# Pooled and local attention with a gated product on one core: five per-engine issue orders replaced by five others

## The chip, the cores and the metric

One Trainium2 chip, one of its cores. The metric is the device time of one execution in microseconds (us); of several runs the median is given. The engines are named as in the profile: PE (TensorE matmul), PEld (its weight loads), DVE (VectorE), ACT (ScalarE), POOL (GpSimd) and SP (SyncE, which here only issues DMAs). L880 is line 880 of the kernel.

## What is computed

Shapes: batch 8, heads 8, sequence 576, head dimension 64; all inputs fp32. Four weights (512x1024, 512x1024, 1024x1024, 1024x512) come as 64-bit floats.

```python
q_d, k_d, v_d = (x.reshape(B, H, Sd, 4, D).mean(axis=3) for x in (q, k, v))
out_up = np.repeat(sm_attn(q_d, k_d, v_d), 4, axis=2)      # pooled attention, 144 keys
mask = np.abs(pos[:, None] - pos[None, :]) < 4             # local attention, 7 keys
out_local = softmax(where(mask, scale * q @ k.T, -1e9)) @ v
x = (out_up + out_local).transpose(0, 2, 1, 3).reshape(4608, 512)
out = (((x @ w1) * (x @ w2)) @ w3) @ w_out
```

## The kernel before

The product w3 @ w_out is folded into one 1024x512 matrix W' first (`fold`), so that a token costs two gate products and one down product. Every fp32 operand of these is split into a high and a low fp32r part, and each product is three matmuls, high*high, high*low and low*high (L306, L307, L308).

The tokens are worked in three kinds of steps:

- **Weights.** Each 128-row block of a weight is loaded as raw 64-bit words (`raw`, L331, 512 KB, a ring of six buffers early on), turned into fp32 by ACT (L338, L346) and DVE (L350) and joined by DVE (L353); only the join gives the raw buffer back for the next load. Joined blocks of w_out (`wo`) and w3 (`wx`) feed 64 folding products on PE (L388, two matmuls each), whose sums are split into `wphl` (L398, L399). The gate weights follow the same way (L432, L434).
- **Attention of batches 0 and 1** ("group units" 0 to 5): local scores by PE (L719, `se_ps`), softmax, transposes (L689), values (L768, `oe_ps`). It lies in the first 190 us, beside the weights. The local attention of batches 2 to 7 is done by DVE and ACT in units 6 to 23, three to a batch: seven products `pr<-q_t,kv` (L880) and their sums (L893, on ACT L890), a softmax over seven offsets (L905 to L916), seven products `pv` (L947, on ACT L939) that are added into `xl`, on DVE (L957) or by an accumulating DMA issued by POOL (L955, three to a unit, in a chain), a transpose (L961), the addition of the pooled result (L968), and the split into `xh` and `xl` (L978, L982).
- **Pooled attention**, one batch at a time: its v rows are summed four to one by a plain load (L458 to L460, SP) and three accumulating DMAs (L457, POOL), each after the one before has landed; from batch 2 on q and k likewise (L454, L473). 16 rows of the sum are copied to a second place (`vl`, L477 on DVE for batches 0 and 1). Then scores (L534), softmax with a normalization on POOL (L566), transposes (L577), values (L495, `o_ps`, which reads `vs` and `vl`), and a copy to `oup` (L506).
- **The gated product** in nine chunks of 512 tokens. For each of eight column blocks f: 24 gate matmuls into two `pab` banks, a copy by ACT (`a`, L1034), a multiplication by DVE (L1036), the split `gh` (ACT, L1040) and `gl` (DVE, L1045), then 12 down matmuls into four `acc` banks.

All of this is recorded as 3096 tasks, each on one engine with its dependencies. The order of issue is not computed: the table `ORDER` lists for ACT, DVE, PE, Pool and SP the numbers of that engine's tasks in the order in which they go out, and `Plan.order` (which also merges the five lists into the program's text, by assumed costs) takes the next of a list only. An engine issues strictly in that order, so an instruction that waits holds back all that stand behind it on its engine. On SP and POOL this is the order of the DMA issues.

```python
left[e] = [l[k] for w in ORDER[e].split() for a, _, b in [w.partition("-")] for k in range(int(a), int(b or a) + 1)][::-1]
...
            if left[e] and all(j in end for j in self.pre[left[e][-1]] + self.begun[left[e][-1]]):
...
            i = left[e].pop()
```

Of the kernel before, what the change touches and what calls it, by code (L numbers as in the profile page):

```python
# [69 lines left out]
        "0-1 122 118 120 117 121 2-3 90 119 93 91-92 4 94 97 95-96 5-6 98 7-8 99 123 9 125 127-128 126 124 10-11 100 131 101-102 13 12 "  # L70
        "103 105 104 132-133 130 106 111 107-108 110 109 141 134 142 129 112-113 135 137 144 114 143 14 140 139 136 16 15 138 17-18 "
        "115-116 19 145 21 20 146 22-24 26 25 31-32 151 147 33 29 152 27 149 28 150 35 148 34 186 30 187 153 155-156 189 188 157 154 158 "
        "190 159 37 36 160 191 162 161 166 38 165 163-164 40 167-168 39 42 41 192 195 43 194 197 193 49 196 204 202 205 203 199 52 207 "
        "206 198 201 200 169 48 57 174 173 60 51 170 172 171 53 50 180 175 177-178 65 176 209 208 54 179 68 45 55 181-182 47 56 183 59 62 "
        "58 64 63 67 184 66 185 61 69 44 46 70 212 73 72 71 76 75 74 213 77-78 214 79 215 80-81 216 82-84 297 85-86 217 88 87 218 89 "
        "210-211 219 236-237 235 232 234 233 239 244 243 245 238 220 241-242 247 246 240 248-249 221 253 250-252 256 262 259 263 258 257 "
        "260-261 264-265 222 254-255 223 266-267 224 268-269 271 270 274 272-273 275 225-226 298 300-301 299 296 316 315 320 318 302 317 "
        "303 321 325 323 319 326 322 324 227 304 309 308 306-307 276 327 228 305 277 229 328-329 334 330 335 331 336 332 337 333 338 230 "
        "339 278 231 341 345 342 344 343 346 350-351 348 352 279 347 349 311 310 280 312 281 353 313-314 354-359 282 360 414 361 415 362 "
        "416 363 417 364 283 365 390-392 389 388 397 387 393-395 398 340 396 418 413 419 284-285 420 286 425 399 424 421-423 436 435 434 "  # L80
        "400 432 401 287 402 406 403 407 404 288 405 408 366 409 289 431 410 433 437 439 411 441 440 290 438 442 426-427 291 428 443 367 "
        "444 429 445 430 446 292 447 293 448-449 531 450 533 294 451 461-462 457 459 368 458 532 452 369 453 295 454 412 455 534 370 460 "
        "464 468 463 530 466 465 535 467 536 371 469 372 470-474 537 475 373 476 538-539 541-542 540 477 506 505 507 374 508 478 509 375 "
        "479 504 480 544 510-511 513 543 481 514 456 515 376 512 545 377-378 516 546-547 517-519 379 520-521 648 522 649 651 523 650 524 "
        "550 525 551 526 548 527 552 380 528 549 553 482 381 647 483 652 554 653 559 558 556 555 557 654 659 655-656 658 657 560 382 484 "
        "561-563 383 564 661 660 565 567 384 485 568 578 385 566 486 575-576 579 574 577 569 386 583 570 585 662 571 487 572 584 488 581 "
        "580 529 582 586 489 587-588 490 589-591 663 592 664 593 623 621-622 624 594 573 491 595 626 596 625 597 492 627 598 630 628 632 "
        "629 631 763 493-495 633 764 767 765-766 634 496 635-640 665 641 668 642 666 643 497 599 667 644 498 645 600 669 499 670 768 675 "
        "769 674 671 673 601 676 672 500 602 677 770 774 772 775 771 773 678 501 679 502 680 603 681 711 682 604 713 715 683-684 712 685 "
        "716 686 605 687 714 688 777 776 689 722 646 778 503 721 720 718 717 719 606 723 607 779-780 608-609 724-728 881 729 882 884 883 "  # L90
        "730-732 610 733 741 737 740 738 742 734 746 735 748 611 739 744 747 612 745 743 690 613 880 885 614 886 749-757 615 758 736 759 "
        "616 760 783 761 691 784 786 617 782 618 781 785 791 619 692 620 790 792 693 887 788 889 888 890 892 891 789 787 694 793-795 800 "
        "796 801 797 802 893-894 798 695 803 895 804 799 762 828 696 830 829 697 832-833 831 836 834 837 839 835 838 698 805 896-897 699 "
        "840 700 841-842 701 843-846 702 847 703 848-850 854 851 856 852 855 859 704 857-858 862-863 865 864 861 860 705 806-807 706 866 "
        "808 867-870 707 871 708 872-873 809 874-875 709 876 810 877 710 853 878 899 898 900 811 902 901 812 903 906 909 905 908 907 904 "
        "813-814 910 815 911-917 879 816 918-922 950 948 817 946 945 818 949 947 954 953 955-956 819 952 951 820 957 821 923 822 973 972 "
        "975 924 981 823 982 979 958 964 959 965 960 824-825 961 966 925 967 962 926 826-827 968 963 969 927 976 974 977-978 928 980 971 "
        "929 983 930 984-986 931 987-988 932 989-995 970 933-936 996 937-943 997 944 998-1015"
    ),
    DVE=(  # L100
        "78-79 82-83 80 84 81 86 85 87 113 88 114-115 0 116 97 102 101 98 103 99 1 117 90 89 91 94 92-93 104 95 2 105 96 3 106 118-122 4 "
        "127 123 5-6 128 7 129 107-108 130 124 109 125-126 8-9 160 110 161 111 134 112 162 135-136 164 137 165-166 131-133 100 10-12 "
        "138-140 13-14 141 15 143 142 16 144 17-18 159 19 163 145-147 20 148 25-26 152 27 153 23 154 21-22 171 170 28 172 155 24 167 173 "
        "168 149 169 150-151 174-175 156 176 157 194 183 182 177 184 158 195-196 29 197 185-187 30-31 181 198 178 199 179 200 32 201 180 "
        "33 205 34 206 35 207-208 202-204 189 188 190 44 209-211 40 42 51 191-193 43 41 218 216 214 212 215 213 45 37 46 39 47 49 52 48 "
        "54 53 56 55 58 50 57 36 38 59 61 60 220 63 62 221 65 64 66-67 222-223 68-72 224 73 75 225 76 74 77 226 217 219 227 236-239 "
        "243-246 240-242 247-250 252 251 253 228 254-255 229 256 261 257 262-267 230 258-260 231 268 270 269 271 232 276 272 274 278 273 "
        "275 277 279 298 233 297 299-300 309 301 311 302 313 234 296 312 310 314 316 315 303-304 317 305 319 318 320 235 321-323 280 "
        "324-325 306 326 307 327 308 281 328 330 339 341 340 342-343 329 282 344 332 345-347 331 333 335 349 283 350 348 284 351 334 352 "
        "285 353-357 359 384 414-415 385 416 358 336 386 286 388 417 389 287 418 387 419 337 391 360-361 390 362 364 392 394 338 395 393 "  # L110
        "288 420 396 421 289 422 397 363 398 426 399 428 427 400 430 401 429 423 365 424 402 425 403 290 405 431 291 366 433 292 404 432 "
        "407 293 367 434 436 408 406 437 410 294 435 295 438-444 409 445 447 456 458 533 532 457 534 446 460 449 411 459 368 412 461 369 "
        "462 450 463 370 413 535 448 536 371 537 452 464 466 465 467-468 451 469 372 470-473 373 538-539 474 540 502 476 453 504 506 541 "
        "505 542 374 543 454 503 375 507 475 509 508 510 512 511 513 478 376 455 477 377 479 481 378 514-516 379 517-520 480 651 650 523 "
        "521 544 652 545-546 548 547 522 549 525 550 653 380 654 482 381 655 483 526 524 551 528 552 554 553 656-657 555 658 484 556 485 "
        "557 527 558 382 659 559 660 560 661 561 383 562-563 565 574 529 576 486 578 577 487 575 564 579 567 580-582 584 583 488 530 489 "
        "566 585 568 570 531 586-587 490 588-590 569 491 591-592 594 620 622 624 623 571 593 572 492 596 621 493 625 627-628 494 626 573 "
        "630 597 595 629 599 495 631 496 632 767 633 768 497 634 769 635-638 598 639 641 498 662 770 664 666 600 640 601 643 663 665 499 "
        "602 771 667 500 772 669 642 501 644 646 668 603 670 672 671 673 774 674 645 604 675 773 676 605 677 775 678-679 708 680 709 681 "
        "710 712-713 606 776 683 777 647 607 648 682 714 685 778 711 715 608 716 686 717-718 649 719 684 688 720-721 609 722-725 610-611 "  # L120
# [1096 lines left out]
```

## Time and profile before

| | us |
|---|---|
| three runs | 819.39, 821.57, 822.07 |
| their median | 821.57 |
| the profiled execution, its own time | 821.9 |
| its span, first to last instruction | 819.8 |
| PE busy / DVE busy / ACT busy / POOL busy in the span | 757.4 / 613.3 / 518.3 / 153.6 |
| mean granted TensorE clock, as a share of full speed | 0.965 |

How to read the views: the page's second part cuts the span into 40 slices of 20.5 us and gives a digit for each; a table of stretches gives busy time by engine, the mean granted clock, the busy share of the 16 DMA engines and the data rate; the timeline lists instructions with start, duration and, in brackets, the idle time of the engine before them and what ended it; the list of waits sums such idle times; the chain that ended last follows back, from the last instruction, what released each step. Matmul records overlap their successors, so their starts tell the rate.

### The profile page before, as it was taken

Reading aid. Unit: us, or ns where it says so; the run is one execution under the profiler, and the core shown is the slowest. Engines: PE = TensorE matmul, PEld = TensorE weight load, DVE = VectorE, ACT = ScalarE, POOL = GpSimd, SP = SyncE. Lnnn points to the kernel's source line nnn. Section 1 sums busy time; section 2 is a strip of 40 time slices with the busy share of each in tenths; the row PEclk is TensorE's granted clock in tenths of the full one; section 3 lists DMA queues with packets and bytes.
Section 4 is the critical chain, followed back from the end, with each engine's and each line's share of the span. In section 5 each row is a group of like instructions: output and inputs, shape, how many; then the busy total and the mean of one; then the engine's idle time right before and its main releaser. Section 6 shows DMA issues by size and latency. Waiting matters only on the chain.

```text
span 819.8 us, 13615 instructions
## 1 busy us (share of the span) xinstructions
PE 757.4 (92%) x4672; PEld 573.7 (70%) x4672; DVE 613.3 (75%) x1047; ACT 518.3 (63%) x2033; POOL 153.6 (19%) x187
## 2 busy tenths in 40 slices
PE   3979889999888999898989899998999999999995
PEld 1435458787666867676768687776788888888884
DVE  5748575647999989999799698998799995841111
ACT  3857785655876867878686496688577757422111
POOL 1212113001223332252141423201011100100000
PEclk9979989999998999999989899999999999999998
DMA  6969796012877687778855478643445342421001
GB/s 210 316 175 288 226 247 169 18 36 79 208 170 185 115 217 173 156 137 210 197 91 141 134 153 186 141 98 109 116 116 131 94 116 72 87 38 52 1 0 52
DMA packets 51964, 111.81 MB, mean 136 GB/s; under 512 B 6056, under 2 KB 20392, under 8 KB 51896
## 3 DMA queue, kind: packets, MB, share of 16 engines
q0 software_dynamic: 15360, 38.94, 27.7%
q1 hardware_dynamic: 36400, 71.75, 27.1%
q8 instruction: 37, 0.61, 0.3%
q14 instruction: 31, 0.25, 0.1%
q10 hardware_dynamic: 136, 0.26, 0.1%
HBM read 80.26 MB, written 9.44 MB: 109 GB/s over the span
## 4 chain that ended last, share of the span: by engine, by line
PE 45%; DMA 22%; DVE 15%; issue 7%; ACT 7%; POOL 3%; SPq 1%; POOLq 0%; DVEq 0%; ACTq 0%
PE pab L306 9%; PE pab L308 9%; PE pab L307 9%; DMA vs<-in_v_dram 7%; DMA xl<-pv 6%; PE acc L308 4%; DMA qks<-in_qk_dram 4%; PE acc L306 4%; PE acc L307 4%; DVE pr L880 4%; DVE s_t L893 2%; PE accw L388 2%; DVE pv L947 2%; PE o_ps L495 1%; POOL pexp L566 1%
## 5 line engine op out<-in xcount | busy, mean ns | idle before, releaser
L939 ACT ACTIVATE pv<-kv,s_t 128x64 f32<-128x64 f32 x432 | 116.1, 340 | 21.3 <-DVE s_t L916 12.6
L890 ACT ACTIVATE junk<-pr 128x64 f32<-128x64 f32 x432 | 110.6, 256 | 22.5 <-DVE pr L880 11.6
L308 PE MATMUL acc<-wphl,gl 128*128 128x512 f32 x288 | 115.0, 399 | 5.7 <-DVE gl L1045 5.5
L306 PE MATMUL acc<-wphl,gh 128*128 128x512 f32 x288 | 116.4, 404 | 2.1 <-ACT gh L1040 2.1
L880 DVE TENSOR_TENSOR pr<-q_t,kv 128x768 f32<-128x768 f32 x126 | 116.9, 951 | 1.6 <-DMA q_t<-in_q_dram 1.4
L307 PE MATMUL acc<-wphl,gh 128*128 128x512 f32 x288 | 113.5, 394 | 0.0
L955 POOL DMA_DIRECT2D xl<-pv x54 | 48.5, 899 | 312.6 <-DVE xl L957 228.4
L1036 DVE TENSOR_TENSOR a<-pab,a 128x512 f32<-128x512 f32 x72 | 49.2, 683 | 68.5 <-PE pab L308 54.2
L1040 ACT CAST gh<-a 128x512 fp32r<-128x512 f32 x72 | 44.4, 617 | 67.6 <-DVE a L1036 40.2
L1034 ACT COPY a<-pab 128x512 f32<-128x512 f32 x72 | 42.0, 583 | 66.3 <-PE pab L308 57.0
L893 DVE TENSOR_REDUCE s_t<-pr 128x12 f32<-128x768 f32 x90 | 83.5, 942 | 0.0
L890 ACT ACTIVATION_READ_ACCUMULATOR junk<-pr 128x1 f32 x432 | 80.9, 187 | 0.0
L1045 DVE TENSOR_TENSOR gl<-a,gh 128x512 fp32r<-128x512 f32 x72 | 51.1, 710 | 29.0 <-ACT gh L1040 28.8
L947 DVE TENSOR_TENSOR pv<-kv,s_t 128x768 f32<-128x768 f32 x72 | 69.3, 971 | 1.3 <-DMA xl<-pv 1.1
L308 PEld LDWEIGHTS acc<-wphl,gl 128*128 128x128 f32 x288 | 54.8, 190 | 21.3 <-DVE gl L1045 9.3
L388 PE MATMUL accw<-wo,wx 128*128 128x512 f32 x128 | 64.1, 643 | 4.7 <-DVE wx L353 4.6
L306 PEld LDWEIGHTS acc<-wphl,gh 128*128 128x128 f32 x288 | 54.8, 190 | 16.2 <-ACT gh L1040 3.7
L306 PE MATMUL pab<-xh,wo 128*128 128x512 f32 x144 | 59.6, 414 | 4.1 <-ACT a L1034 2.8
L307 PEld LDWEIGHTS acc<-wphl,gh 128*128 128x128 f32 x288 | 54.9, 190 | 11.0
L307 PE MATMUL pab<-xl,w1a 128*128 128x512 f32 x144 | 58.5, 406 | 3.3 <-DVE xl L982 3.3
L306 PE MATMUL pab<-xh,w1a 128*128 128x512 f32 x144 | 60.0, 417 | 1.3 <-ACT a L1034 0.7
L457 POOL DMA_DIRECT2D vs<-in_v_dram x48 | 43.2, 969 | 95.3 <-DMA vs<-in_v_dram 70.6
(122 smaller groups left out, 1624.7 us busy)
## 6 DMA issues: line engine op xcount, KB each, us to landing
xl<-pv POOLq DMA_DIRECT2D x54, 384.0 KB, 4.2
raw<-in_w_dram SPq DMA_DIRECT2D x32, 512.0 KB
qks<-in_qk_dram POOLq DMA_DIRECT2D x18, 576.0 KB, 6.4
kv<-in_kw_dram SPq DMA_DIRECT2D x18, 576.0 KB
kv<-in_vw_dram SPq DMA_DIRECT2D x18, 576.0 KB
out_dram<-o_sb SPq DMA_DIRECT2D x28, 256.0 KB
q_t<-in_q_dram SPq DMA_DIRECT2D x18, 384.0 KB
raw<-in_wout_dram SPq DMA_DIRECT2D x8, 512.0 KB
```

Of the source, the lines that this page charges most:

```text
L306: nc.tensor.matmul(out_ps, lhsT=lh, rhs=rh, start=first, stop=False)
L307: nc.tensor.matmul(out_ps, lhsT=lh, rhs=rl, start=False, stop=False)
L308: nc.tensor.matmul(out_ps, lhsT=ll, rhs=rh, start=False, stop=last)
L388: nc.tensor.matmul(accs[m], lhsT=T["x"][:, at:at + 128], rhs=whole(j), start=j == 0, stop=j == NF - 1)
L880: (nc.gpsimd if o in share["qk_pool"] else nc.vector).tensor_tensor(out=T[o], in0=T["q"], in1=T["k"][:, o * D:o * D + nq].rearrange("p (t ...
L890: nc.scalar.activation(out=junk, in_=T[o][:, t], func=AF.Copy, accum_out=T["s"][:, t, o:o + 1])
L893: reds.append(add("DVE", dve_us(nq), lambda o=o: nc.vector.tensor_reduce(out=T["s"][:, :, o], in_=T[o], op=ALU.add, axis=AX.X), [tp], uses ...
L939: nc.scalar.mul(out=T["pv", o][:, tt], in_=T["v"][:, (tt + o) * D:(tt + o + 1) * D], mul=T["s"][:, tt, o:o + 1])
L947: nc.vector.tensor_tensor(out=T["pv", o], in0=T["v"][:, o * D:o * D + nq].rearrange("p (t d) -> p t d", d=D), in1=T["s"][:, :, o].unsqueez ...
L955: t = add("Pool", 0.55, lambda o=o: nc.gpsimd.dma_start(out=T["x"], in_=T["pv", o], accum_op=ALU.add), [t, tm], uses=[hx, h], late=dma_us( ...
L1036: tg = add("DVE", dve_us(size), lambda f=f: nc.vector.tensor_tensor(out=T["a", f], in0=T["p", 1, f][:, :size], in1=T["a", f], op=ALU.mult) ...
L1045: nc.vector.tensor_tensor(out=T["gl", f], in0=T["a", f], in1=T["gh", f].bitcast(F32), op=ALU.subtract)
```

## The change

Only the five number lists of `ORDER` differ. No task, buffer, dependency, assumed cost or other line does; each list is a permutation of the same numbers, 1016 on ACT, 1021 on DVE, 718 on PE, 168 on Pool and 173 on SP. The new lists come from a layout that used the transfers' durations as traced. Cut to a line or two:

```diff
     PE=(
-        "70 64 0-3 71 65 72 6 66 4 7 5 9 8 10 73 12 14 74 11 67 15 75 68 13 76 69 19 17-18 16 23 20 77 21 25 24 22 26 78 30 28-29 85 27 "
+        "70 64 0-3 6 4-5 7 9 65 8 11 10 14-15 12 71 66 13 72 16 18 73 17 20 22 74 21 19 23 27 26 25 75 24 67 76 68 28-33 36 34 69 37 41 "
...
     SP=(
-        "40-42 0 45 1 47-49 43-44 2-5 46 6-7 56-57 8-14 50-51 15-17 52 18 62 59 58 60 19-21 61 22-24 53-55 25-29 80 30-31 63-65 32-35 81 "
+        "40-42 0-3 47 4-5 45 48-49 6-7 43-44 8 46 9-13 56 14 57 15-20 50 21 51 22-23 52 24-25 62 58-61 26-28 53-55 29-31 80 32 63-64 "
...
```

**First place: PE up to the first pooled values.** PE, from the middle of the first half of the fold to the pooled values of batch 0 (`o_ps`). Before:

```order
L388 MATMUL accw<-wo,wx 128x512 x2
L689 MATMUL te_ps<-ident,se 72x128 x6
L388 MATMUL accw<-wo,wx 128x512
L577 MATMUL t_ps<-ident,pexp 128x128 x6
L388 MATMUL accw<-wo,wx 128x512
L689 MATMUL te_ps<-ident,se 72x128 x6
L577 MATMUL t_ps<-ident,pexp 128x128 x3
L388 MATMUL accw<-wo,wx 128x512
L768 MATMUL oe_ps<-pte,v_w 32x64 x48
L495 MATMUL o_ps<-pt,vs 32x144 x8
```

and now:

```order
L388 MATMUL accw<-wo,wx 128x512 x6
L689 MATMUL te_ps<-ident,se 72x128 x6
L388 MATMUL accw<-wo,wx 128x512
L577 MATMUL t_ps<-ident,pexp 128x128 x6
L768 MATMUL oe_ps<-pte,v_w 32x64 x48
L577 MATMUL t_ps<-ident,pexp 128x128 x3
L388 MATMUL accw<-wo,wx 128x512 x8
L495 MATMUL o_ps<-pt,vs 32x144 x8
```

Ahead of the first `o_ps` matmul stood 16 of the 64 folding products; now 36 do. SP's list moved with it: the first four weight loads now follow directly on the first three attention loads, where two of them stood behind twelve `v_w` loads.

**Second place: DVE around the copy of `vl` for batch 0** (L477), which waits for the last of the accumulating DMAs. Before:

```order
L747 TENSOR_SCALAR emx<-emx 128x6
L613 TENSOR_TENSOR qks<-qks,q_283 128x144 x2
L751 TENSOR_SCALAR esm<-esm 128x6
L752 RECIPROCAL esm<-esm 128x6
L753 TENSOR_TENSOR se<-se,esm 128x432
L477 COPY vl<-vl 16x512
L350 TENSOR_SCALAR raw<-raw 128x512
L353 SCALAR_TENSOR_TENSOR wo<-wo,raw 128x512
L353 SCALAR_TENSOR_TENSOR wx<-wx,raw 128x512
```

and now:

```order
L753 TENSOR_TENSOR se<-se,esm 128x432
L353 SCALAR_TENSOR_TENSOR wx<-wx,raw 128x512
L399 TENSOR_TENSOR wphl<-accw,wphl 128x512
L350 TENSOR_SCALAR raw<-raw 128x512
L399 TENSOR_TENSOR wphl<-accw,wphl 128x512
L353 SCALAR_TENSOR_TENSOR wx<-wx,raw 128x512
L399 TENSOR_TENSOR wphl<-accw,wphl 128x512 x2
L477 COPY vl<-vl 16x512
L353 SCALAR_TENSOR_TENSOR wx<-wx,raw 128x512 x2
```

Eight joins of weights (L353) stood ahead of the copy; now 18 do. The copy for batch 1 moved in the same way, from ahead of the first gate-weight block's join to behind the third's.

**Third place: DVE around the first accumulating add of unit 6.** The add is issued by POOL after the first of the two L957 and must have landed for the second. Before:

```order
L957 TENSOR_TENSOR xl<-xl,pv 128x768
L1036 TENSOR_TENSOR a<-pab,a 128x512
L880 TENSOR_TENSOR pr<-q_t,kv 128x768
L947 TENSOR_TENSOR pv<-kv,s_t 128x768
L893 TENSOR_REDUCE s_t<-pr 128x12
L880 TENSOR_TENSOR pr<-q_t,kv 128x768 x2
L957 TENSOR_TENSOR xl<-xl,pv 128x768
```

and now:

```order
L957 TENSOR_TENSOR xl<-xl,pv 128x768
L893 TENSOR_REDUCE s_t<-pr 128x12
L947 TENSOR_TENSOR pv<-kv,s_t 128x768
L1036 TENSOR_TENSOR a<-pab,a 128x512
L880 TENSOR_TENSOR pr<-q_t,kv 128x768 x2
L893 TENSOR_REDUCE s_t<-pr 128x12
L539 TENSOR_REDUCE gmx<-s_ps 128x3
L1045 TENSOR_TENSOR gl<-a,gh 128x512
L880 TENSOR_TENSOR pr<-q_t,kv 128x768 x2
L540 TENSOR_SCALAR gnb<-gmx 128x6
L947 TENSOR_TENSOR pv<-kv,s_t 128x768
L957 TENSOR_TENSOR xl<-xl,pv 128x768
```

Six instructions lay between the two L957, five of them of the long kind (128x768); now twelve do, eight of the long kind.

## Rows read from the trace of the kernel before

**Rows 1.** The page's slices of 20.5 us: DVE busy and granted clock in tenths.

```profile
DVE  5748575647999989999799698998799995841111
PEclk9979989999998999999989899999999999999998
```

**Rows 2.** Table of stretches: us, busy us and count by engine, PEclk, DMA share, GB/s.

```profile
0.00:43.90 43.90, 28.17 (x299) 15.13 (x299) 26.19 (x85) 28.38 (x103) 8.86 (x25) 1.00 0.88 262
43.90:57.10 13.20, 8.01 (x71) 3.91 (x72) 8.00 (x18) 7.15 (x16) 2.50 (x3) 0.61 0.49 118
57.10:117.60 60.50, 55.60 (x531) 27.76 (x529) 42.80 (x109) 44.64 (x138) 10.54 (x12) 0.97 0.90 254
117.60:188.50 70.90, 69.93 (x663) 55.98 (x663) 41.34 (x94) 38.88 (x110) 7.71 (x9) 0.97 0.36 96
188.50:610.20 421.70, 394.30 (x2235) 306.24 (x2234) 380.82 (x579) 310.55 (x1355) 112.76 (x125) 0.96 0.64 148
610.20:742.90 132.70, 132.69 (x580) 108.56 (x579) 100.99 (x148) 75.70 (x292) 11.19 (x13) 1.00 0.38 89
```

**Rows 3.** Timeline, DVE and PE, where the seventh chunk (number 6) begins.

```profile
609.50 0.68 DVE L982 TENSOR_TENSOR xl<-xt,xh 128x512 fp32r<-128x512 f32 x1
...
610.82 0.39 PE L306 MATMUL pab<-xh,w1a 128*128 128x512 f32 x1
```

**Rows 4.** The chain that ended last, 15 to 60 us: start, duration, what.

```profile
19.93 9.41 DMA vs<-in_v_dram
...
29.64 7.31 DMA vs<-in_v_dram
...
37.23 6.55 DMA vs<-in_v_dram
...
45.28 3.77 DMA vs<-in_v_dram
```

**Rows 5.** Timeline, DVE: the two copies of `vl`.

```profile
47.72 0.42 DVE L477 COPY vl<-vl 16x512 f32<-16x512 f32 x1 [6.97 <-DMA vl<-in_v_dram]
...
89.28 0.42 DVE L477 COPY vl<-vl 16x512 f32<-16x512 f32 x1 [5.90 <-DMA vl<-in_v_dram]
```

**Rows 6.** Timeline, SP: two weight loads that follow each other.

```profile
35.13 0.37 SPq L331 DMA_DIRECT2D raw<-in_w_dram  x1
49.42 0.34 SPq L331 DMA_DIRECT2D raw<-in_wout_dram  x1
```

**Rows 7.** Timeline, PE: first pooled values, folding products, and the first gate matmul.

```profile
49.09 1.19 PE L495 MATMUL o_ps<-pt,vs 128*32 128x144 f32 x16 [5.21 <-DMA vs<-in_v_dram]
...
60.31 4.13 PE L388 MATMUL accw<-wo,wx 128*128 128x512 f32 x9
...
117.58 0.80 PE L306 MATMUL pab<-xh,w1a 128*128 128x512 f32 x1 [0.55 <-ACT oup L506]
```

**Rows 8.** Waits of DVE: us in total, times, longest us.

```profile
DVE xl L957 <- DMA xl<-pv: 9.3, 6, 4.1
...
DVE xt L961 <- DMA xl<-pv: 2.9, 2, 1.9
```

**Rows 9.** Timeline, DVE: the first add of unit 6, and the longest wait for one.

```profile
226.69 0.96 DVE L957 TENSOR_TENSOR xl<-xl,pv 128x768 f32<-128x768 f32 x1 [1.07 <-DMA xl<-pv]
...
409.15 0.96 DVE L957 TENSOR_TENSOR xl<-xl,pv 128x768 f32<-128x768 f32 x1 [4.11 <-DMA xl<-pv]
```

**Rows 10.** Timeline: pooled values of batch 4 (PE), and their first use (DVE).

```profile
347.93 0.70 PE L495 MATMUL o_ps<-pt,vs 128*32 128x144 f32 x16
...
417.84 0.95 DVE L968 TENSOR_TENSOR xt<-xt,oup 128x768 f32<-128x768 f32 x1
```

**Rows 11.** Timeline: POOL's normalization of two batches, and the transposes after one.

```profile
313.62 1.55 POOL L566 TENSOR_TENSOR pexp<-pexp,grs 128x288 f32<-128x288 f32 x2
...
450.72 5.92 POOL L566 TENSOR_TENSOR pexp<-pexp,grs 128x288 f32<-128x288 f32 x2 [3.50 <-DVE grs L557]
...
456.69 1.33 PE L577 MATMUL t_ps<-ident,pexp 128*128 128x128 f32 x5 [4.07 <-POOL pexp L566]
```

168 rows, old and new, of tables (ACT, DVE, PE, Pool) are left out of this document.

## The prediction

> **What bounds the kernel now.** I read the slices of the page first. The digits of DVE stand at 8 or 9, with three exceptions, from the eleventh slice to the thirty-third, and the granted clock falls below 9 in two slices of the first 123 us and in three beside pooled work later [rows 1]. Then I cut the span where the work changes [rows 2]: the first gate matmul (117.6 us), the end of the local attention of batches 0 and 1 (188.5), the landing of the operands of chunk 6 (610.2), the first matmul of the last chunk (742.9). The reader is to see that the bound changes from stretch to stretch.
>
> From 610.2 us on it is PE alone: 132.69 of 132.7 us busy. Its first gate matmul of chunk 6 starts 0.6 us after DVE has finished the low half it reads [rows 3]. So the end is that moment plus about 210 us (819.8 - 610.2), which no order can shorten much, since PE already runs without a gap.
>
> From 188.5 to 610.2 it is DVE: 380.82 of 421.7 us busy, 40.9 idle. PE, with 394.30, is not idle either, but it lives from the tokens that DVE finishes.
>
> Before 117.6 us no engine is full. DMA is busy for 0.88, 0.49 and 0.90 of the three stretches, that is 38.6 + 6.5 + 54.5 = 99.6 us of 117.6 [rows 2]. In the middle stretch everything sags at once: PE is busy for 8.01 of 13.2 us, at a clock of 0.61. The chain of waits says why: one load and then three accumulating DMAs for the pooled values of batch 0, each after the other, 9.41, 7.31, 6.55 and 3.77 us long as the chain passes them [rows 4]. Two engines stand still for the last of them: DVE 6.97 us at the copy of `vl` [rows 5], and PE 5.21 us at the first pooled values [rows 7]. DVE's wait costs twice: behind the copy stand the joins that give raw buffers back, and SP, which issues in order, sends no weight from 35.5 to 49.42 us [rows 6]. The same copy waits 5.90 us for batch 1 [rows 5].
>
> **The change part by part.** Nothing is added or removed: every instruction, DMA and buffer is the same, and no duration is changed by the edit itself. Only waits can go or come.
>
> *The first gate matmul.* Ahead of PE's first pooled values now stand 36 folding products instead of 16. Nine such matmuls take 4.13 us at full clock [rows 7], so the twenty products more (two matmuls each) take some 18 us, over three times the wait that they have to cover. On DVE, ten more joins stand ahead of the copy, so the raw buffers return during the wait and SP goes on loading. So I take the whole wait of 5.21 us as gone. With it goes the slow clock of that stretch. A mean of 0.61 between the levels 1 and 0.5 (2.4 and 1.2 GHz) means 10.3 of the 13.2 us at the lower one; 5.21 of the stretch are the wait, so of PE's 8.0 us of work between 5.1 and 8.0 ran at half speed, which cost 2.6 to 4.0 us; I take 3.3. The copy for batch 1 is moved too, and its 5.90 us come before the gate weights; but PE had products left to do then, so between 0 and 5.9 of it reaches PE, and I take 1.5. Sum: 5.2 + 3.3 + 1.5 = 10 us.
>
> Its bounds: nothing, if the loads bind anyway; 18 us, if the 99.6 us of DMA ran without a gap. At the 0.90 of the third stretch the same transfers need 110.7 us, a gain of 7; so 10 asks for a busy share of 99.6 / 107.6 = 0.93, a little more than the trace has shown. It carries over to the end of the next stretch, where PE is busy for 69.93 of 70.9 us and so passes a shift on.
>
> Here a rule speaks against the change. The rows show four links of 3.8 to 9.4 us [rows 4]. The Trainium skill ("DMA: Bandwidth & Descriptors", section "Anatomy of one DMA — SWDGE (gpsimd) path") gives a DMA issued by POOL about 2.0 us plus its bytes over 436 GB/s; by that the largest part of a link (144 KB) would take, as an estimate, 2.3 us. By this rule three links would end well before the copy and the term would be 0, the time 816. The rows disagree threefold, beside a full weight stream, and the measurement decides.
>
> *The units, 188.5 to 610.2 us.* DVE's waits for accumulating adds come to 9.3 + 2.9 = 12.2 us [rows 8]. Whether a wait goes is read off the order with durations: for unit 6 the work between the two L957 was five long instructions at about 0.96 us and one short one of under 0.7, some 5.4 us, and DVE then waited 1.07 [rows 9]; now eight long and four short ones make about 9.7 us, so that wait is covered. Counted in the same way for all 54 adds, the cover is larger for 35, smaller for 16. For the longest wait, 4.11 us [rows 9], it is 5.3 us where it was 5.6, so that one may stay. I take half of the 12.2, 6 us; the ends are 0 and 12. The other idle time of DVE hangs on PE, ACT and small steps; I cost it at nothing either way.
>
> *What becomes later.* The pooled batches now come later, nearer to their use. Worst is batch 4: its values started at 347.93 us and were first used at 417.84, 69.9 us later [rows 10]. Now 216 more gate and down matmuls stand ahead of them, at 132.7 / 580 = 0.229 us each 49 us [rows 2]. Some 20 us of cover are left, so I cost it at nothing; if the cover went, each us would stand on DVE. POOL's list has the adds and the pooled sums interleaved in another way; POOL is busy for 112.76 of 421.7 us, and an add behind a pooled sum waits for one issue, under 1 us. No part of the tail is moved in a way that counts: PE's last stretch stays full.
>
> The sum: 821.9 - 10 - 6 = 805.9 us against the profiled execution's own time (span 819.8 and 2.1 around it). The median of the runs is 0.3 lower, so **806 us**.
>
> **The rivals.** *The loads bind.* If the prologue's transfers are the limit, the waits only change their place, and 0 to 3 us are left there. For it: the shares of 0.88 and 0.90, and SP's new list, which asks for weights sooner, beside the same accumulating DMAs. Against it: the 0.49 of the middle stretch, where DMA itself stood idle since nothing was asked of it. Time: 821.9 - 2 - 3 = 817.
>
> *All of it comes.* 18 us in the prologue and 12 in the units, about 792. Against it: it needs transfers without a gap.
>
> *POOL's normalization becomes the wait: slower.* Two L566 take 1.55 us at 313.62 us and 5.92 at 450.72, with the same shapes, and PE's transposes wait 4.07 for the latter [rows 11]; the granted clock of the slice then stands at 8 instead of 9 or more [rows 1], some 3 us more. Such an event costs about 7.5 us. The mechanism is POOL beside DVE products that both read SBUF, and the order decides what stands beside it; twelve pairs are placed anew. From two more such events than before (15 us) the gain is used up; with three more the time is 805.9 + 22.5 = 828. For it: the new layout used the transfers' durations, not this; DVE is as dense as before. Against it: one pair of twelve was so long. The Trainium skill ("SBUF — State Buffer", section "SBUF: two separate sides") has it as a rule that a VectorE instruction with two SBUF inputs and a GpSimd instruction that reads SBUF exclude each other; the pair at 450.72 agrees.
>
> That the change does nothing is excluded: each engine issues in its list's order, and the rows of the order differ.
>
> **How the numbers follow.** A difference of 0.3%, 2.5 us, is about what a measurement of this kernel can tell from none. Forecast 0.58, all of it faster (its own range 797 to 814); all of it comes 0.12, faster; the loads bind 0.14, of which 0.07 faster, 0.06 the same and 0.01 slower; the slow normalization 0.16, slower. Together faster 0.77, same 0.06, slower 0.17. The range leaves out the ends of the second and the fourth case: 790 to 826.
>
> **What would show it.** Right: in the profile after, the first gate matmul starts near 107 us; neither copy of `vl` waits more than 2 us; PE has no wait at the first pooled values and the clock stays at full speed there; SP issues weights without a hole of over 5 us; DVE's waits for adds come to some 6 us; chunk 6 starts near 595. Wrong: a first gate matmul after 115 us with a DMA share over 0.9 (the loads bind), two or more L566 pairs of over 4 us with transposes waiting behind them, a wait of DVE at L968 for the pooled result, or PE waiting for tokens after chunk 6.

## The result, and the profile after

The change makes the kernel faster: 784.34 us (median of four runs, 781.96 to 785.73) against 821.82 (819.39 to 823.44) of the kernel before in the same comparison, a ratio of 0.9543 with a 95% interval of 0.9509 to 0.9578. That is 37.5 us; 16 were forecast, and the time lies 5.7 us below the range given. The profiled execution took 785.7 us, with a span of 784.0 and a mean granted clock of 0.998. All times and ratios here and below are of fast runs: a few executions, over 1.5% above the fastest of the same kernel, are left out.

The slices of the page after, DVE and granted clock, which answer to [rows 1]:

```profile
DVE  6666876648998999899999899999999998411211
PEclk9999999999999999999999999999999999999999
```

No slice falls below 9 any more. The table of stretches after, cut at the same events as [rows 2]; columns: busy us (and count) of PE, PEld, DVE, ACT, POOL, then granted clock, busy share of the DMA engines and GB/s (a DMA packet is counted whole where it starts, so the share of a short stretch can pass 1):

```profile
0.00:43.90 43.90, 31.16 (x203) 14.89 (x204) 28.05 (x83) 26.56 (x85) 8.81 (x25) 1.00 0.93 283
43.90:57.10 13.20, 12.10 (x132) 6.61 (x131) 8.62 (x24) 13.17 (x40) 2.47 (x3) 1.00 1.05 282
57.10:105.05 47.95, 44.26 (x565) 22.97 (x563) 37.90 (x104) 38.15 (x120) 8.35 (x10) 1.00 0.83 236
105.05:174.60 69.55, 65.56 (x646) 51.51 (x647) 42.03 (x96) 41.89 (x122) 9.34 (x11) 1.00 0.41 105
174.60:573.80 399.20, 384.15 (x2250) 298.86 (x2249) 383.12 (x583) 306.88 (x1357) 109.67 (x125) 1.00 0.68 158
573.80:710.30 136.50, 135.98 (x594) 111.06 (x594) 100.97 (x147) 75.91 (x292) 11.14 (x13) 1.00 0.37 87
```

The reader is to see two gains of different size. The first gate matmul comes at 105.05 instead of 117.58 [rows 7], 12.5 us earlier, and the units begin 13.9 us earlier (174.6 for 188.5). The stretch of the units is 399.2 us long instead of 421.7, a gain of 22.5. From its end to the end of the span it takes 784.0 - 573.8 = 210.2 us where it took 209.6: nothing there.

In the units PE is busy 10.2 us less for nearly the same matmuls (384.15 for 394.30) at a granted clock of 1.00 instead of 0.96, and idle 12.4 us less (15.0 for 27.4). DVE does the same work (383.12 for 380.82) and is idle 16.1 us instead of 40.9; 24.8 less idle and 2.3 more busy make the 22.5. The waits of DVE in this stretch, before (us in all, times, longest):

```profile
DVE a L1036 <- PE pab L308: 9.5, 6, 3.3
DVE gmx L539 <- PE s_ps L534: 7.8, 5, 3.7
DVE xl L957 <- DMA xl<-pv: 7.8, 5, 4.1
...
DVE xt L961 <- DMA xl<-pv: 2.9, 2, 1.9
DVE gl L1045 <- ACT gh L1040: 2.2, 4, 1.0
```

and after:

```profile
DVE xl L957 <- DMA xl<-pv: 2.9, 3, 2.2
...
DVE gmx L539 <- PE s_ps L534: 1.0, 1, 1.0
DVE xt L961 <- DMA xl<-pv: 0.8, 1, 0.8
...
DVE a L1036 <- PE pab L308: 0.5, 1, 0.5
```

The waits for accumulating adds (L957, L961) fell from 10.7 to 3.7 us. The three that hang on PE's products and scores (L1036 and L539 directly, L1045 through ACT's copy of the product) fell from 19.5 to 1.5: 18 us that the forecast had left at nothing.

### The profile page after: what moved, and what is told of

Same layout as the page of the kernel before. It is cut to its first block, busy times and chain, and to the rows that moved or that the text cites. A ratio compares the mean times of both kernels' runs of the same rounds, so it can differ in the third digit from the quotient of the medians.

```text
span 784.0 us, 13611 instructions
## 1 busy us (share of the span) xinstructions
PE 739.1 (94%) x4672; PEld 559.8 (71%) x4672; DVE 613.1 (78%) x1047; ACT 515.1 (66%) x2033; POOL 149.8 (19%) x187
## 4 chain that ended last, share of the span: by engine, by line
PE 47%; DVE 23%; DMA 15%; ACT 7%; issue 5%; POOL 1%; SPq 0%; DVEq 0%; POOLq 0%; ACTq 0%
PE pab L306 9%; PE pab L308 9%; PE pab L307 9%; DVE pr L880 6%; PE acc L306 5%; PE acc L308 5%; DMA raw<-in_w_dram 5%; PE acc L307 5%; DMA xl<-pv 4%; DVE s_t L893 3%; DVE pv L947 2%; DVE xl L957 2%; PE accw L388 2%; DMA q_t<-in_q_dram 2%; DVE a L1036 1%
## 5 line engine op out<-in xcount | busy, mean ns | idle before, releaser
L880 DVE TENSOR_TENSOR pr<-q_t,kv 128x768 f32<-128x768 f32 x126 | 119.9, 976 | 3.1 <-DMA kv<-in_kw_dram 2.2
L1036 DVE TENSOR_TENSOR a<-pab,a 128x512 f32<-128x512 f32 x72 | 49.0, 681 | 64.8 <-PE pab L308 63.4
L1045 DVE TENSOR_TENSOR gl<-a,gh 128x512 fp32r<-128x512 f32 x72 | 49.2, 683 | 27.4 <-ACT gh L1040 27.2
L457 POOL DMA_DIRECT2D vs<-in_v_dram x48 | 48.0, 1091 | 102.1 <-DMA vs<-in_v_dram 86.7
L306 PE MATMUL pab<-xh,w1a 128*128 128x512 f32 x144 | 57.3, 398 | 2.9 <-ACT a L1034 1.8
L306 PE MATMUL pab<-xh,w2a 128*128 128x512 f32 x144 | 57.1, 397 | 2.8 <-DVE a L1036 2.8
```

The source lines that it names most:

```text
L306: nc.tensor.matmul(out_ps, lhsT=lh, rhs=rh, start=first, stop=False)
L880: (nc.gpsimd if o in share["qk_pool"] else nc.vector).tensor_tensor(out=T[o], in0=T["q"], in1=T["k"][:, o * D:o * D + nq].rearrange("p (t ...
L1036: tg = add("DVE", dve_us(size), lambda f=f: nc.vector.tensor_tensor(out=T["a", f], in0=T["p", 1, f][:, :size], in1=T["a", f], op=ALU.mult) ...
L1045: nc.vector.tensor_tensor(out=T["gl", f], in0=T["a", f], in1=T["gh", f].bitcast(F32), op=ALU.subtract)
```

## Experiments: are the two gains independent?

In all runs below only number lists of `ORDER` are edited, unless a diff shows otherwise; in the profiles of a few, line numbers are 1 to 3 higher, since more lines stand ahead of them there. First, hybrids. `h_ba` takes the order of before for all that started before 188.5 us and that of after for the rest (DVE's list where they part):

```diff
-279 298 233 297 299 300 309 301 311 302 313 234
+279 298 297 299 300 301 302 309 311 313 233 310
```

> The order of before for every step that started before 188.5 us in its trace, and the order of after for all the rest. Theory A (the two stretches gained independently of each other: 13.9 us up to the units, 22.5 us in them): 188.5 + 399.2 + 210 + 2 = 800 us, within 797 to 803. Rival B (the units only gained because they were entered in another state, with other loads and pooled batches under way): 810 or more. Rival C (nearly all of the gain belongs to the units, and the early lead would have been lost again anyway): under 792.

Measured: 801.31 us, ratio 0.9773 (0.9727 to 0.9819). `h_ab` is its mirror image:

```diff
-277 279 232 298 297 299 300 301 302 309 311 313
+277 232 279 298 233 297 299 300 309 301 311 302
```

> The mirror image: the order of after up to 174.6 us of its trace, the order of before for the rest. Theory A: 174.6 + 421.7 + 210 + 2 = 808 us, within 805 to 811. Rival B: under 800. Rival C: 816 or more, since the units of before would wait the lead away.

Measured: 809.30 us, ratio 0.9875 (0.9824 to 0.9925). The waits of DVE in the units, first of `h_ba`, then of `h_ab`:

```profile
DVE xl L960 <- DMA xl<-pv: 4.7, 2, 4.2
...
DVE a L1039 <- PE pab L311: 0.5, 1, 0.5
```

```profile
DVE xl L959 <- DMA xl<-pv: 12.0, 4, 5.6
DVE a L1038 <- PE pab L310: 9.9, 7, 3.3
DVE gmx L541 <- PE s_ps L536: 4.9, 3, 2.6
```

Both times lie where theory A put them: 800 and 808 were expected from adding the stretches. Each part gains by itself, and the waits belong to the order of the units, not to how they are entered. How exactly the parts add up is less certain: the spans of the traces give 21.4 and 12.9 of the 35.8 us, but the ratios 2.3% and 1.3% of 4.6%, and the 8.6 us that are missing there are a little more than the intervals allow for.

## Experiments: the early stretch

`p_undo` puts one thing back in after: the copy of `vl` for batch 0 (100) stands again behind 133, PE's first pooled values (69) behind 68, and ACT's copies of these accordingly.

```diff
 DVE
-161 133 162 17 110 111 18 112 19
+161 133 100 162 17 110 111 18 112 19
 PE
-76 68 28 29 30 31 32 33 36 34 69
+76 68 69 28 29 30 31 32 33 36 34
```

> In after, only the copy of vl for batch 0 is put back to where before has it (behind the normalization of the second local scores, 22 instructions of DVE earlier), with PE's first pooled values 8 folding products earlier and ACT's copies of them accordingly. Theory A: DVE waits about 8 us at the copy again, the joins behind it and the weight loads that need their buffers come late, and the time rises by 4 to 10 us, to 788 to 795; the slow clock comes back beside it. Rival (load order): 783 to 787.

Measured: 796.58 us, 12 above after's 784.34 and a little more than was expected. The timeline, one row each from DVE, SP, PE and PE again (start, duration, in brackets the idle time before):

```profile
54.49 0.42 DVE L479 COPY vl<-vl 16x512 f32<-16x512 f32 x1 [9.49 <-DMA vl<-in_v_dram]
...
41.94 14.31 SPq L333 DMA_DIRECT2D raw<-in_w_dram  x2
...
55.90 1.22 PE L390 MATMUL accw<-wo,wx 128*128 128x512 f32 x1 [11.01 <-DVE wx L355]
...
116.59 0.79 PE L308 MATMUL pab<-xh,w1a 128*128 128x512 f32 x1
```

The chain of the prediction is all there: the copy waits 9.5 us, SP has two loads in 14.3 us since no raw buffer returns, PE stands still for 11.0, and the first gate matmul falls back from 105.05 to 116.6. So the late place of the copy, with what reads it, is necessary. Is it sufficient? `p_alone` moves it in before, behind four joins more, with PE's values behind six products more and ACT's copies accordingly; the copy for batch 1 (181) goes behind the third gate join.

```diff
 DVE
-132 133 100 10 11 12 138 139 140 13 14 141 15 143
+132 133 10 11 12 138 139 140 13 14 15 100 16 141
 PE
-13 76 69 19 17 18 16 23 20 77
+13 76 19 17 18 16 23 20 69 77
```

> In before, only the copy of vl for batch 0 is moved behind joins 11, 12, 13 and 15 (four more), PE's first pooled values and ACT's copies of them behind six more folding products, the sums that read them behind one more join, and the copy of vl for batch 1 behind the third gate join. SP's list is that of before. Theory A (the two copies and what stands behind them are what the early part lost): the waits of 7.0 and 5.9 us at the copies fall under 2, PE has no wait of 5 us at its first pooled values and no slow clock there, the first gate matmul moves from 117.6 to 108 to 112 and the time is 812 to 817. Rival (the order in which SP asks for weights at the start made the difference): 819 to 822, the first gate matmul at 116 or later.

Measured: 817.52 us, ratio 0.9979 (0.9945 to 1.0012). Its copy for batch 0 and its first gate matmul:

```profile
50.35 0.42 DVE L480 COPY vl<-vl 16x512 f32<-16x512 f32 x1 [0.69 <-DMA vl<-in_v_dram]
...
117.96 0.80 PE L309 MATMUL pab<-xh,w1a 128*128 128x512 f32 x1 [0.15 <-ACT oup L509]
```

The wait is gone and nothing arrives: from 57.1 us on this run had a granted clock of 0.90, and PE was busy for 55.92 of the 60.9 us up to the first gate matmul. With SP's first loads put in after's order as well (`sp_copy`; the scores that read the sums of batch 0 also go behind seven folding products more, 77 on PE and three steps of DVE), it was no better.

```diff
 SP
-42 0 45 1 47 48 49 43 44 2 3 4 5 46
+42 0 1 2 3 47 4 5 45 48 49 43 44 46
```

> In before, the later copies of vl as in the run before that had them alone, the scores that had to wait for the sums of batch 0 placed behind seven more folding products, and SP's first loads in the order of after (four weight blocks before the v_w loads). Theory A1 (it takes both: weights ahead at the start, and copies that don't stop the joins): first folding product at 14.3, first gate matmul at 107 to 112, time 810 to 815. Rival (a third thing binds, the chain of the second pooled batch through ACT and PE up to its values at 114): first gate matmul at 116 to 118, time 815 to 820.

Measured: 823.65 us, ratio 1.0003 (0.9968 to 1.0038). Its first folding product started at 21.95 us, after 9.37 of waiting for a join, not at 14.3: DVE's list still had the join behind a step that read `k`, whose load now stood behind the weights (DVE waited 6.35 us for it). A1 falls; the first gate matmul, at 118.43, is about where the rival had it.

What the two lack can be counted in the traces. Folding matmuls of PE up to 57.1 us (busy us and count, PEld, clock, DMA share, GB/s), of 128 in all, in before, `p_alone`, `p_undo` and after:

```profile
0.00:57.10 57.10, 22.87 (x39) 8.66 (x40) 0.91 0.79 229
...
0.00:57.10 57.10, 24.65 (x44) 8.96 (x44) 0.94 0.85 247
...
0.00:57.10 57.10, 26.19 (x50) 10.09 (x51) 0.93 0.87 256
...
0.00:57.10 57.10, 33.80 (x67) 13.11 (x68) 1.00 0.96 283
```

By then DVE has done 14, 13, 14 and 18 joins (`sp_copy`: 44 matmuls, 13 joins). So the lead of after at this point is folding done ahead, out of weights loaded and joined sooner; a wait that goes without more joins brought 5 of these 28 matmuls and no time. And the chain to the first gate matmul of before, `p_alone` and `sp_copy` has the rival's end with a weight load in it: a join at 102 to 103 us lets a load go (6.4, 7.8 and 8.2 us), and ACT stands 1.1, 2.5 and 2.9 us for it ahead of its copies for batch 1's pooled values. After's chain has no load behind 80 us. No run moved that step of ACT alone.

## Experiments: one thing at a time in the units

`u_later` gives DVE's readers of PE's results more room, in before:

```diff
 DVE
-302 313 234 296 312 310 314 316 315 303 304 317
+302 313 296 312 234 310 314 316 315 317 303 304
```

(234 is an L1036, 303 and 304 are L539.)

> In before, between 188.5 and 610.2 us, 46 of 64 DVE instructions that read a result of PE (the products of L1036 and the maxima of L539) stand one long instruction (0.96 us) later; L1045 follows where it would come closer to its L1036. Nothing else moves. Theory A (DVE and PE wait for each other because each consumer stands too close behind its producer; the waits of DVE for PE were the larger part of what the units lost): by the trace the 15.8 us of such waits become 8 to 10, and the time falls by 4 to 8 us, to 814 to 818, with fewer spells of the slow clock. Rival B (the adds by DMA were the loss): no change within 2 us. Rival C (the delayed products starve PE's down matmuls): slower than before.

Measured: 833.71 us, ratio 1.0153 (1.0104 to 1.0201). Waits in its units, DVE and then PE:

```profile
DVE xl L957 <- DMA xl<-pv: 17.5, 8, 5.3
DVE grs L556 <- ACT pexp L549: 7.8, 3, 5.7
DVE a L1036 <- PE pab L308: 6.2, 4, 3.7
DVE gmx L539 <- PE s_ps L534: 5.2, 3, 2.2
...
PE pab L306 <- DVE a L1036: 16.7, 10, 5.2
PE acc L308 <- DVE gl L1045: 9.9, 10, 2.3
```

It is slower, as rival C had it, and more by the gate matmuls than by the down matmuls that it named. DVE waits less for PE's products and scores (11.4 us for 17.3), but PE waits 16.7 us for the bank that the late L1036 holds (3.2 before) and 9.9 for `gl` (5.5), and DVE itself longer for the adds (17.5 for 7.8) and for ACT. A product has to stand after the end of its gate matmuls and before PE needs the bank again, and a shift that helps at one end of this window hurts at the other.

`u_earlier` takes room away, in after (234 and 280 are L1036):

```diff
 DVE
-233 310 312 234 314 316 315 317 235 319 318 320 296
+233 310 234 312 314 316 315 317 235 319 318 280 320 296
```

> In after, between 174.6 and 573.8 us, 60 of 66 of the same DVE instructions (L1036 and L539) stand one long instruction earlier; L1045 stays. Theory A: the waits of DVE for PE, 1.2 us now, come to about 8.6 more, PE is held up less or not, spells of the slow clock may return, and the time rises by 5 to 12 us, to 789 to 797. Rival B: within 2 us of after. Rival C (earlier products feed PE sooner): faster than after.

Measured: 793.87 us, 9.5 above after, as theory A had it; in its units (after: 0.5 and none):

```profile
DVE a L1036 <- PE pab L308: 6.2, 6, 2.5
DVE a L1036 <- ACT a L1034: 4.6, 7, 1.7
```

`u_adds` moves only the readers of the accumulating adds, in before (331 and 334 are L957):

```diff
 DVE
-346 347 331 333 335 349 283 350 348 284 351 334
+346 347 333 331 335 349 283 350 348 284 351 352
```

> In before, in the same stretch, only the DVE instructions that read the landing of an accumulating add (second and third L957, L961, the L947 that reuses the buffer) stand later: for 34 of 41 adds, with DVE work between raised from a median of 6.6 us towards 9. Theory A: the 10.7 us of waits for these transfers fall to 3 to 6, the time by 2 to 6 us, to 816 to 820. Rival B (the adds were the loss in the units): 806 to 811.

Measured: 825.62 us, ratio 1.0032 (0.9988 to 1.0077): no gain, neither theory's. What the waits for adds are worth it doesn't tell, for they did not go: in the one trace kept (an execution of 837.33 us) they come to 13.9 us in the units, and the waits of L1036 to 12.0. More cover in DVE's list alone bought nothing.

`u_fill` asks about the clock. Of before, it keeps the order and adds matmuls of zeros where PE stood still ahead of a slow spell.

```diff
+FILL = {153: 10, 208: 8, 306: 9, 310: 12, 326: 10, 515: 14, 588: 7, 246: 5, 258: 4, 284: 5}
...
+            into = [x for x in held.values() if x is not None][:1] if t in fill else []
+            for x in into * fill.get(t, 0):
+                nc.tensor.matmul(x[:, :128], lhsT=zero, rhs=ident, start=False, stop=False)
             t.fn()
```

> Before with 79 short matmuls (128x128, a zero block added into an open acc bank, so that no result changes) put on PE ahead of nine of the steps of the units at which PE stood still for 1.2 to 4.1 us and after which the slow clock came. They take about the time that PE waited. Theory K (the slow clock is a cause of its own: PE waits, falls to 1.2 GHz, delivers late, and DVE waits for it): the spells of the units, 34 us in all, fall under 12, the waits of DVE for PE from 15.8 to under 9 us, and the time to 806 to 816. Theory W (what counts is how much of the other engine's work stands between a gate product's end and the reuse of its bank; the clock is a companion): 818 to 824.

Measured: 816.75 us, ratio 0.9978 (0.9941 to 1.0014). The units of before in the table of stretches, from the first product of unit 6 to the first gate matmul of chunk 6:

```profile
193.30:610.80 417.50, 390.10 (x2204) 303.15 (x2203) 379.66 (x574) 307.79 (x1345) 112.76 (x125) 0.96 0.64 148
```

the same of `u_fill`, the group of its filling matmuls (busy us, mean ns; two records to a matmul), and its waits of DVE from 193 to 610 us:

```profile
197.10:608.00 410.90, 394.17 (x2363) 310.89 (x2362) 376.80 (x574) 307.31 (x1345) 114.82 (x125) 1.00 0.65 150
```

```profile
L1151 PE MATMUL acc<-ident,zero 128*128 128x128 f32 x158 | 19.3, 276 | 0.0
```

```profile
DVE xl L957 <- DMA xl<-pv: 12.8, 5, 5.1
DVE a L1037 <- PE pab L308: 6.0, 2, 3.3
DVE gmx L539 <- PE s_ps L534: 4.4, 3, 2.2
```

The clock stays at full speed, and without the 19.3 us of filling PE is busy for 374.9 us, 15 less. The time hardly follows: it lies between the ranges of the two theories, and within the interval of no change. The units of this trace are 6.6 us shorter than those of before's, but in `p_alone`, which has the order of before there and no filling, they take 411.4 us, so the trace alone shows no gain. So the 10.2 us that PE's work shrank by in after are not by themselves a gain of 10; that PE would else have spent most of the time waiting is the likely reading. The interval still allows some 5 us, and the fillers may cost something where the wait had become shorter.

## Experiments: the lists laid out anew

If DVE's list can't be moved alone, all five together should do. Here the units' lists were laid out anew, by single moves kept when they shortened the order's length with the traced durations. `s_dve` does it for DVE's list alone, `s_all` for all five lists of before, `s_after` for those of after. Their lists begin to differ so:

```diff
 DVE (s_dve)
-277 279 298 233 297 299 300 309 301 311 302 313
+277 279 233 298 297 299 300 301 302 309 311 234
 PE (s_all)
-142 234 146 123 170 171 124 148 235 172
+142 234 123 124 148 146 147 170 235 149
 PE (s_after)
-120 121 142 234 123 122 124 143 148 235
+120 121 143 234 148 142 123 147 145 122
```

> Before, with DVE's list alone laid out anew between 188.5 and 610.2 us (each instruction moved singly, by the traced durations, with landings of 5 to 6 us for the adds and 4 to 5 for loads); the lists of PE, ACT, POOL and SP are those of before. Theory W: DVE can only make the best of the windows that PE's order leaves (median 3.9 us in before, 6.2 in after), so a part of the 22.5 us comes: 805 to 814. Rival D (DVE's list was the whole fault): under 803. Rival N (one list alone gives nothing): 818 or more.

> Before, with all five lists laid out anew in the same stretch, in the same way; up to 188.5 us it is before. Theory W: as much as in the hybrid with the units of after, or more: 783 to 800, with windows of 5 us or more, waits of DVE for PE under 4 us and few slow spells. Rival (the units of after hold something that durations alone don't give): 803 or more.

> After, with all five lists laid out anew from 174.6 us to the end, in the same way: is there a version that beats both? Theory W: PE still stands still for 15 us of the units and DVE for 16, so 768 to 780. Rival (PE and DVE are as full as an order can make them, and real durations scatter): 781 to 788.

Measured: `s_dve` 830.33 us, ratio 1.0156 (1.0095 to 1.0218); `s_all` 820.55, 1.0009 (0.9965 to 1.0053); `s_after` 798.77, 0.9760 (0.9690 to 0.9829), 14 above after by the times and 18 by the ratios. Three misses, and one reason is seen in the units of `s_after`, in the waits of DVE and, for the longest, in the timeline of SP and DVE:

```profile
DVE pr L880 <- DMA kv<-in_kw_dram: 17.3, 7, 6.7
DVE pr L880 <- DMA q_t<-in_q_dram: 8.6, 4, 3.5
```

```profile
410.43 0.48 SPq L863 DMA_DIRECT2D kv<-in_kw_dram  x1
...
423.32 0.96 DVE L880 TENSOR_TENSOR pr<-q_t,kv 128x768 f32<-128x768 f32 x1 [6.70 <-DMA kv<-in_kw_dram]
```

The layout had the loads land 4 to 4.8 us after issue; this one took 423.3 - 410.4 = 12.9. `s_after`'s order was good against PE and ran into the loads, 25.9 us of waits where after has 2.7 on L880. Its units are 8.6 us longer than after's (402.4 for 393.8); another 6.9 us are lost behind them, since this layout went on to the end (216.8 us from chunk 6's first gate matmul to the end of the span, 209.9 in after). So the same was done with longer landings:

```diff
 landing after issue, us     (two values, both laid out for)
-loads of q, k, v: 4, 4.8    adds: 5, 6
+loads of q, k, v: 8.5, 12   adds: 5.5, 8
```

> As s_all (before up to 188.5 us, all five lists laid out anew from there to 610.2), but with loads of q, k and v for a unit taken at 8.5 to 12 us from issue to landing and the adds at 5.5 to 8, as the waits of the runs so far show them, where s_all had 4 to 4.8 and 5 to 6. Theory L (the windows gain only if the transfers' real times are laid out with them): the 38 us of waits for loads in s_all fall under 12, and the time to 785 to 805. Rival (single moves only push the idle time about): 813 or more.

> As s_after (after up to 174.6 us, the units laid out anew), with the same longer landings. Theory L: waits for loads fall from 26 us to under 8, and the time to 772 to 786, against 784 of after. Rival: 790 or more.

> As s_dve (only DVE's list of the units laid out anew), with the longer landings. Theory L and W together: one list can shorten the waits a little but not widen the windows: 808 to 819. Rival N (one list alone against four others of another layout loses): 822 or more.

Measured: `s_all2` 813.08 us, ratio 0.9875 (0.9850 to 0.9900); `s_after2` 788.03, 0.9578 (0.9533 to 0.9623); `s_dve2` 832.93, 1.0125 (1.0086 to 1.0165). One list alone loses again, now with `DVE a L1036 <- PE` back at 18.6 us. The other two ran the units themselves quickly: from the first L880 of unit 6 to the first gate matmul of chunk 6 it takes 399.8 us in `s_all2` and 388.1 in `s_after2` (417.5 before, 393.8 after), but both began them 6 to 10 us late. The last two leave the beginning alone: the new layout sets in at 204 us of before (`s_all4`) or 190 of after (`s_after4`).

```diff
 DVE (s_all4)
-316 315 303 304 317 305 319 318 320 235 321
+316 315 317 319 318 320 321 322 323 235 324
 PE (s_after4)
-172 173 149 150 151 152 154 155 153 236
+172 173 151 150 149 152 174 153 236 176
```

> Before up to 204.0 us, and the units from there to 610.2 us laid out anew with the longer landings. Theory L: entry as in before (193), units 397 to 402 us, time 800 to 807, close to the 801 of the hybrid that has the units of after. Rival: 811 or more.

> After up to 190.0 us, and the units from there to 573.8 us laid out anew with the longer landings. Theory L: entry as in after (unit 6's first product at 180), units 388 to 392 us long, time 776 to 783, below after's 784. Rival (the scatter of the landings takes back what single moves give): 784 or more.

Measured: `s_all4` 798.91 us, ratio 0.9710 (0.9666 to 0.9755), 22.5 us below before with before's early stretch; `s_after4` 782.69, 0.9512 (0.9468 to 0.9557), which can't be told from after's 0.9543, and its units, 395.0 us in the trace, are not shorter than after's 393.8. The units of `s_all4` in the table of stretches, and its waits of DVE there:

```profile
194.90:585.00 390.10, 377.50 (x2204) 295.95 (x2203) 376.27 (x579) 306.24 (x1347) 112.96 (x125) 0.99 0.69 159
```

```profile
DVE pr L880 <- DMA kv<-in_kw_dram: 2.6, 2, 1.7
DVE a L1036 <- PE pab L308: 2.3, 3, 1.3
DVE gmx L539 <- PE s_ps L534: 0.9, 1, 0.9
...
DVE xl L957 <- DMA xl<-pv: 0.3, 1, 0.3
```

Starting from before, five lists laid out together with the loads' real times give what the change gives in the units (390.1 us for 393.8), and by the same sign: waits for PE, for adds and for loads are all small at once. The width of the window for L1036, from the end of its gate matmuls to the moment PE is free for the next ones into the same bank, is no condition: counted from the starts and ends in the traces, its median is 5.7 us in before (40 products), 6.0 in after (42) and 5.4 in `s_all4` (41); the 3.9 and 6.2 of the expectations did not come out of this count. So theory W falls in that part. Nor does the product's place in the window tell a good order: at the median it starts 1.8, 3.1 and 1.4 us behind the window's opening. That the place matters within a given order is what `u_later` and `u_earlier` show; one measure that tells a good order from a bad one was not found, nor was an order that clearly beats after.

## Why the prediction was right or wrong

**The bound by stretches** held. The last stretch kept its 210 us, and chunk 6 starts when the low half is ready: at 574.09 us, not near 595.

**The first gate matmul**: forecast 107, measured 105.05. Neither copy waits, PE goes into the first pooled values without a pause and at full clock. The size of the term (12.5 for 10) was nearly right. Its working, 5.2 + 3.3 + 1.5 us from three waits, was not: with the copies' waits gone and the rest of before's order kept (`p_alone`), the first gate matmul stayed at 118.0. That the size came out is luck in this part. The late copy is a condition (`p_undo`: 11.5 us lost there), and the other lists have to use it for more joins and folding, 18 and 67 by 57.1 us where before has 14 and 39. Which list gives how much was not separated. The bound by DMA had a wrong premise: it took the same transfers to lie ahead of the first gate matmul, and only some 94 us of them do (0.93, 1.05 and 0.83 of the three stretches), so that 12.5 us came at a mean share of 0.90. That SP would issue weights without a hole of over 5 us was not true: 9.4, 8.2 and 13.1 us lie between weight loads from 11.1, 63.4 and 73.3 us on, in part filled with other loads. The hole of 14.3 us that the copy had made [rows 6] is gone; from 25 to 54 us none is over 5.3.

**The rule against it.** Of the four links [rows 4] the first, 9.41 us, is SP's load; the three that POOL issues took 7.31, 6.55 and 3.77 us. By the rule of the Trainium skill ("DMA: Bandwidth & Descriptors", section "Anatomy of one DMA — SWDGE (gpsimd) path") the term would have been 0; the measurement decides against that: with the copy back at its early place in `p_undo`, two of these links take 6.7 and 5.9 us in the chain, and DVE waits 9.5 us for the last.

**The units** are the step that failed, in these words: "The other idle time of DVE hangs on PE, ACT and small steps; I cost it at nothing either way." The term was 6 us for the adds; their waits fell about as forecast, by 7.0 in the stretch and from 12.2 to 6.4 over the whole span, from which the 12.2 had been read (10.7 of it lies in the units). The stretch gained 22.5, and 18 us of the 24.8 that DVE's idle time fell by were waits for PE's products and scores. I had looked at cover for the adds alone, though the same count (what stands between a result and its reader) could be made for every pair of engines. The runs also show that waits can't be taken away one kind at a time: `u_adds` gave cover to the adds and their waits stayed, `u_later` gave it to PE's results and lost 12 us to waits on other engines. What is gained is gained by a whole order in which no wait only moves elsewhere. That each of the 18 us is paid for by one place in the lists is not shown.

**The rivals.** POOL's normalization did not become the wait: the longest pair of L566 in the units takes 3.21 us, where 5.92 stood before [rows 11], and the transposes wait 2.0 us for POOL in all instead of 4.6. The loads did not hold the gain back: the middle stretch went from a DMA share of 0.49 to 1.05. They may be what sets the first 57 us now, at a share of 0.96; no run tests that. "All of it comes" (792) was nearest, for another reason than its own, and the time still came out below it. Batch 4's pooled values start at 380.48 us and are first used at 392.35, 11.9 us later where some 20 were forecast [rows 10], and caused no wait at L968.

## What to carry to other kernels

Where every engine issues in a fixed order, read the waits in both directions between each pair of engines, and ask of a new order whether both sides of each buffer (producer done, reader in time for the reuse) and the transfers have room at once. A wait taken away in one list alone mostly comes back elsewhere. Here five lists moved together gained 22 us, where moves of DVE's list alone gained nothing or lost (in the units no other list was tried alone), and where all five laid out for landings of 4 to 6 us gained nothing either. Lay out with landings measured in the kernel under its own traffic, longer ones among them.

## What the runs showed of the hardware

- The traffic's own spread. Where DVE waited for a 576 KB load of k, its instruction started 6.5 to 12.9 us after the load's issue (median 7.7 of 26 such waits in the traces of seventeen kernels; loads that nobody waited for are not in this count). The accumulating adds of 384 KB, whose median to landing the profile of after gives, for the units, as

```profile
xl<-pv POOLq DMA_DIRECT2D x41, 384.0 KB, 4.5
```

  took 3.9 to 12.2 us where DVE waited (120 waits). The first layouts had counted on 4 to 6 us for both.
- In the units of before PE is idle for 27.4 us and the granted clock is 0.96; with matmuls of zeros in nine of its pauses (`u_fill`, the same order) the clock is 1.00 and PE's own work takes 15 us less. The time changed by 0.2%, within the interval of no change. So in this order the low level looks more like a sign of waits than a cost of its own, with the reserve that the filling may cost something too.
